# Two heads' chunk states by one whole-array product, in a retention and token-mixer kernel on one core

## The chip, the core and the metric

The kernel runs on one core of a Trainium2 chip. The metric is the device time of one execution in microseconds (us); the median of several executions is compared. A profile of one execution gives the busy time of every engine, the transfers, and which instruction waited for which. The engines are TensorE (PE; its weight loads are listed as PEld), VectorE (DVE), ScalarE (ACT), GpSimd (POOL) and SyncE (SP). They run side by side and meet at semaphores.

## The reference, cut to what matters

Four sequences (B = 4) of S = 768 tokens have H = 8 heads of D = 64 columns. The first half is a linear attention with a decay per head, the second half an MLP mixer over tokens and then over channels.

```python
gamma = 1.0 - 2.0 ** (-5.0 - np.arange(H))
for t in range(S):
    state = gamma * state + np.einsum('bhd,bhe->bhde', k[:, :, t], v[:, :, t])
    y[:, :, t] = scale * np.einsum('bhd,bhde->bhe', q[:, :, t], state)
x = y.transpose(0, 2, 1, 3).reshape(B, S, H * D)
h = np.maximum(x.transpose(0, 2, 1) @ w_tok1, 0) @ w_tok2
u = x + h.transpose(0, 2, 1)
out = u + np.maximum(u @ w_ch1, 0) @ w_ch2
```

## The kernel before, in words

**Fronts.** The 8 heads of a batch b are taken in 4 pairs p, two heads side by side in 128 columns; a pair is written (b,p) below. `front(b, p)` does one pair. The 768 tokens are 6 chunks of 128. Inside a chunk the attention is a masked 128x128 product; from chunk to chunk a 64x64 state per head is carried. The steps are, with their lines:

- k (and, in some pairs, q) is multiplied by its decay on ACT or DVE (L533, L535), and both are turned so that head columns lie on partitions: by PE (L559, L561, copied out of the bank by L569 or L574) or by a transposing transfer.
- **State products (L587 to L593).** For each of the first 5 chunks and each of the two heads, one PE product k'v of a 64x64 result (L591): 10 products into one PSUM bank. Head 0 takes the left 64 columns of the PE array and partitions 0 to 63, head 1 the right 64 columns and partitions 64 to 127. An operation that divides the array in this way has `tiled="col"`. The score products (L642) divide it by rows (`"row"`), and some of the turns of q (L559) by columns too (`"turn"`); everything else uses the whole array.
- **Recurrence (L595 to L606).** The first chunk's state is copied from the bank to U (L601, on ACT or DVE). Then four DVE steps (L603) form U[c] = decay * U[c-1] + bank[c], each 128 partitions x 64 columns, and each needs the step before it.
- U is scaled into the two diagonal blocks of `cross` (L621 on ACT or L623 on DVE, one instruction for each head).
- Score products (L642), the causal mask (L653, DVE, four instructions of 128x384 for each pair), the products with v (L673) and the products with `cross` (L699) give y in two banks. These are copied to x (L715).
- The token mixer follows: L730, its ReLU (L739 on ACT, L741 on DVE), L750, and copies to u and to X (L715); u is turned for the channel mixer (L795 with L801, or a transfer).

**Backs.** `back(b)` does the channel mixer of a batch. Batch 0 has plain products at L829. The others, and the second layer of all, use a seven-product scheme for 2x2 blocks: L898 for the first layer, L1051 and L1061 for the second, with sums on DVE (L868, L1015), copies out of a bank (L909, L1041) and adds (L918, L1068). L977 and L986 do what is left over of the last batch. At the very end one product group is cut in two halves that write the two halves of the columns of one bank (L1104); the two halves are then added to X one after the other (L1068), and stored.

**What sets the order.** Every piece of work is an `Op` with one or two ways (an engine and a planned cost each). All `Op`s are numbered as they are made. The string `ORDERED` lists these numbers, two base-62 digits each, in the planned order of start; `WAYS` has one digit for each number that picks the engine. `arrange` (L111) keeps each engine's list in that order, gives each `Op` a PSUM bank or a buffer, and L1190 to L1198 emit the instructions in the planned order. Engines run their lists strictly in order. While PE would be idle before 21 us, filler products of zeros are issued (L1196). Loads go through the POOL queue (L475, L492, L495), stores through SP or ACT (L992, L1090).

The state products need k with its decay and v (`kl + [vl, ...]`), and nothing else of the pair. The bank that holds them is free again after the last step of the recurrence. U has 2 buffers, so two pairs can be between their first copy and `cross`.

Of the kernel before, what the change touches and what calls it, by code (L numbers as in the profile page):

```python
# [9 lines left out]
FP = mybir.dt.float32  # L10
# [100 lines left out]
def arrange(ops, BANKS, seq, ways):  # L111
# [147 lines left out]
    "0e0c070d01080f05000h0306090g0i1h1i1l0m0a1j0j1k0b1m1V0n1W1v1w0k1R1x1S1y1A1T0l1z1n1U1B1o0o2r2s25261p2t1q0p292u"  # L259
    "1r2v2a1s1C0q311t322w0r1u3528331D361E1F0t1X1Y27342G1Z2K0s1G2F202x21222J2b232y2I240x1H2H2d2z2c1I0u2e2A2L2f2B2C"  # L260
    "3f2g1J0w2D3h1M1K2h2E3i1N0v372i1L2N2M382O2P392j0y1O3a2m3b2Q3g3c4L3j3d2R0D3k3e2k3l3m2S3n0A3o2n2T3p2l1P3q2W0z2U"
    "1Q3r2X2V2p0B4M3s2Z2o3t2Y3w0C303u5k3B4d3x3C3F2q490H3z4a3v3D3A4b4ead4cag3GaeaN0EaO3Eb23yaPavaf5lb30Faw3Paxah3Q"
    "aQ0Gaias3Tb4aR3SaZaSb03R0N4nb13H4p4f3Iap4qay3Jaq3Kaj4rar0Iaz4g3L3Vat3MaA4o3UaKau0R3NaLaB4h4iakaC3Oam4j4Han4k"
    "3WaE1dao3X0JaFalaH3Y02aIaD1fbhaMbk3ZaT1eaGaUaJ400MaV1gbb41be4Ibnbibc4lbp4204bo4Jbdbl430O4Kbfbm4519bjbr440Kb8"
    "461ab54mb6bsb9bg0Q1baWbaaX474s1cbPb70LaY4u4NbQ4VbJ4Obw4P4Xby4Ybx4Q4t5h5gbAbL0T5S4Rbtbz4w4S0S4v5P4ZbCbubB4xbU"
    "4W0U4Tbq4y4Ubv516q50bF0P4z5Q524A546n4DbD4B53bV5mbE555VbY4CbG4Ec5565n4F6r5T5W5i6sbK57bN5j5o5X585p5YbO48c95q59"
    "5Z5rbSbZ5s60c65Uca5u5tbMcebT5w615R5b5vcfbW5x625zc85BbXci6o5c5y6p7tc1c05D5Acj5CbR0W6t4Gc75Ecn6Y6uc25F0X6v5d6Z"
    "5a6w70cgco5G6x176V6y63ch6z5H640V5e5I655K5fcb66675J686ackcc5L6W6ccd695M6bcl5N0Y6d6Bcm5O6e6D0Z6E716fcr12cvcscM"
    "cw6g6FcNcxcA6hcycRcBcOctcS6jcucD6icUcP6kcC726CcE6m6HcTcV73cFd36lcK7u6AcH6XcWd1cL74dScId2cYcX7vdUd4cZ6G816J75"
    "117zdT7w6I7xd87A766KdX7BdVd910dZd5dY7Cczdb6Ld6e0dcdacGdWe16Mdd82e7e26Ndf84cQdi85e87De486dgdjdk7E6O77e579dl6P"  # L270
    "7y78dB7bdpdC6R7adqdm83d7dG7cds7ddHdrcpdtcJ7edndJ6Qc3dDd0dKdudI6S7ge37fdL7h7idz6U14dEdw7jdQdvdAdxdN16dR7kdedM"
    "6TdFdOe6eX15dh7lev8z7HeYdo877L7p88dPex7mdyez7K7n7IeG7F897o8Aef8aeA8Bew8CeB8beg7qeEeRcq7r7JeV7seF8cey8d8feC7G"
    "eIbH8jeWeH7M7OeJ7N8i7P7QeK13eT7ReZeN8e8g18f297eS9aeO7Sf398e9f07T8h8D8l8neL7UeD8E7Xeb7V8F9df1eU7YekeM7W80f68G"
    "ea7Z9eeled9Fec998k9f8meef48Hf78o9gc4ei9G9hbI8Ieo9if5eh9bf8f9ej9c8p8Jemepfa8q8Ken9HfdeP8Neq8r9j8Q8s8Oer8t8R8L"
    "8v8Pfh8ufyfefi9lesfzfm8w9nfDfn9mfAfEg6fffp8xfBfGfqfo9p8MfjfrfwfHfFfgfx8TfNfk8VfI8SfO8U9L9o8WfK9IfP8XfLft9Mfs"
    "fRfufQ8Y9kfCfSfUg7g89NfV8Z9r9tgb9J9O909Kg9gc9qfX9P91ge9QfY9sfW8ygfgd9ufZg49293ggg5g1fJgl9vg0gnflgmgig2949wgh"
    "gjgo96gE959xgsgagF9T9RfT9ygt9WgJ9z9X9BgKgLg39Ugvgu9VgwgM9SgGgNgpgx9AgCgHgTfv9YgOa0gU9Za1gya2gzgPgqgQgDhJa3hD"
    "gkhHgA9ChFa49EhIhOhEa5gRgIhMfMhPhKa6hNhhhSgBhGhQgrhLhlgShRhja9hmhVhTa7hihnaahWhUach1gVgZh2hYhqgXh0gWfchshrh4"
    "htgYh6h5hkethuhoabh3a8h8hphvh7hwh99DhahxhdhyhzhbhBhZeQhci3iki0i4iSilimi2i8i1i5i9ipheiri6iqibhAiaicinishCiZid"
    "fbitiieuhfifiuijiBigiwiIiCixiziDiTiGiEiUiHiXi7iVj9iYiJieiWjgiviAiKj0jsiLj1kRiQiFiNj2iRj7iOj4j8jbioj5jajqkBhg"  # L280
    "j6jejcjrktjfiPjvj3kCjhjwkujtjijyjxjjjzjojukJjkjljAjpjFjdkKjBjCjmjGk7iMihjDkvk3jEjLiyk4kwjnk5kxk8jHkLkcjMjJke"
    "jIkykfjSjQjTkdkijRkzkgkjkAk6jUkhjWjKjVkkk9jXklkDkEkakFhXjYkMkGjNkbk1kHkNkmkOjZjOkIkPjPknkQk0kqkokSk2kTkUkrkV"
    "kWkpkskXkY"
)
WAYS = (
    "000000000000000000000000000000000000000000000000000000000000000000000000000000001000000000010000000000000000"
    "100000100000001000000000000000000010110100101000000000000000000000000000010000000000000000000000000000000000"
    "110010011010001000011000000000000000000000100000000000000000000000000000000100100010000000000000000000000000"
    "001000000100000000000000000000000000000001001000000000000000000000000001100100000000000000000000000100000110"
    "010010000000000000000000000000001011001000000000000000000000000000001100100000000000000000000000000010000010"  # L290
    "000000000000000000000000000000001000000000000000010100000000101100100000100000000000000000000000000000000000"
    "000000000000000000000000000000000000000000000000000000000000001000000000000001000000000000000000000100000000"
    "000000000000011000000000000000000000000010000000000000000000000000000000001000000000100000000000000001000000"
    "000000000010000000000000000000000000000000000000000000001000000000000000000001000000000000000010000000000000"
    "000000100000000100001000000000100000000010000000000000000100010010000000000000000000000000000000010000000000"
    "000000000001100000100000000100000110000000000000000000000000000000000010100001000000100000000000000001000000"
    "000000000010010000000010000000100000001000000000000001100000000001000100010001000000000000000000000000000000"
    "00001"
# [4 lines left out]
def kernel(  # L303
# [11 lines left out]
    nc = tc.nc  # L315
# [80 lines left out]
    mask = const_p.tile([P, 1, P], FP, name="mask")  # L396
    zero = const_p.tile([P, 384], F16, name="zero")
# [106 lines left out]
    def front(b, p):  # L504
# [19 lines left out]
        def rows_of(j):  # L524
            return slice(j * D, (j + 1) * D)
# [61 lines left out]
        def emit():  # L587
            st = tile_of(ST, [P, 512], FP)
            for c in range(NC - 1):
                for j in range(2):  # L590
                    nc.tensor.matmul(st[rows_of(j), c * D:(c + 1) * D], K.tile[:, c, j], V.tile[:, j, c],  # L591
                                     start=True, stop=True)
        pp = op(one("PE", (179, 347), emit), kl + [vl, two_before], [ST], [K, V], tiled="col")  # L593

        prev = None  # L595
        for c in range(NC - 1):
            def emit(e, c=c):
                u = tile_of(US, [P, NC - 1, D], FP) if c == 0 else US.tile
                st = ST.tile[:, c * D:(c + 1) * D]
                if c == 0:  # L600
                    (nc.scalar.copy if e == "ACT" else nc.vector.tensor_copy)(u[:, 0], st)  # L601
                else:
                    nc.vector.scalar_tensor_tensor(out=u[:, c], in0=u[:, c - 1], scalar=gp[:, p:p + 1], in1=st,  # L603
                                                   op0=ALU.mult, op1=ALU.add)
            prev = op(either(emit, DVE=(190, 276)) if c else either(emit, DVE=(132, 216), ACT=act(D)), [pp, gp_op, prev], [US] if c == 0 else [],
                      ([] if c == 0 else [US]) + [ST])  # L606
# [622 lines left out]
```

## Time and profile before

| | |
|---|---|
| median of 3 runs | 186.15 us (185.56 to 186.44) |
| the profiled execution | 185.28 us, of it a span of 183.5 us in the trace |
| PE busy | 177.1 us (97%) |
| DVE busy | 168.9 us (92%) |
| ACT busy | 137.5 us (75%) |
| POOL busy | 53.8 us (29%) |
| granted PE clock | 1.00 throughout |

A row of a group of instructions reads: line, engine, operation, output<-inputs, partitions x elements and type, count, then total busy us and mean ns of one, then the idle time of that engine ahead of them and what ended it. In a timeline a row is start, length, engine, line and count of a merged run of equal instructions; a product's own length covers its way through the array, so the next product starts long before its end. In the chain of waits, each row is start, length and what the chain ran through.

### The profile page before, as it was taken

To read this page: it belongs to the slowest core of one execution; us is meant where nothing else is said; L and a number is where in the kernel's file an instruction comes from. 1 tells how busy PE (TensorE), PEld (TensorE's weight loads), DVE (VectorE), ACT (ScalarE), POOL (GpSimd) and SP (SyncE) were. 2 spreads that over 40 slices of the span, in tenths; PEclk is the share of its full clock that TensorE was granted. 3 is DMA by queue.
4 is the path that set the end of the run, shared out by engine and by line. 5 is a ranking of instruction groups with operands and counts; after the bars stand their busy time and mean duration, and the time that the engine had idled before them with its cause. 6 is when DMAs were issued, how large, how long until landed. Compare 5 with 4: busy or idle time off the path is not lost.

```text
span 183.5 us, 5308 instructions
## 1 busy us (share of the span) xinstructions
PE 177.1 (97%) x2089; PEld 133.9 (73%) x2089; DVE 168.9 (92%) x450; ACT 137.5 (75%) x320; POOL 53.8 (29%) x63
## 2 busy tenths in 40 slices
PE   7789999999999999999999999999999999999993
PEld 3455898566789988866668899767778986566893
DVE  5699999989999899999999999998999989889893
ACT  6667899547979998899999896899975455688100
POOL 8997586553508008604051220000000000000000
PEclk9999999999999999999999999999999999999999
DMA  6999999999999999999999799702602333610046
GB/s 121 153 173 182 179 187 201 178 193 206 168 155 160 154 162 152 160 153 131 132 211 121 200 118 187 176 0 42 90 2 46 88 126 120 229 57 0 4 184 218
DMA packets 94137, 25.31 MB, mean 138 GB/s; under 512 B 83616, under 2 KB 91296, under 8 KB 94112
## 3 DMA queue, kind: packets, MB, share of 16 engines
q0 software_dynamic: 67728, 13.18, 85.6%
q1 hardware_dynamic: 24656, 9.31, 23.9%
q10 hardware_dynamic: 1728, 2.49, 4.0%
q8 instruction: 16, 0.26, 0.5%
q14 instruction: 9, 0.07, 0.1%
HBM read 26.74 MB, written 6.29 MB: 180 GB/s over the span
## 4 chain that ended last, share of the span: by engine, by line
PE 86%; POOL 5%; DMA 5%; DVE 2%; issue 0%; POOLq 0%
PE bank L898 22%; PE bank L1051 16%; PE bank L1061 12%; PE bank L829 9%; PE bank L750 6%; PE bank L730 6%; DMA wt<-in_moe_w_tok_dram 5%; PE bank L642 3%; PE bank L977 3%; PE bank L673 3%; PE bank L699 2%; PE bank L591 2%; POOL v L495 2%; POOL k L495 2%; POOL q L492 2%; PE bank L795 1%
## 5 line engine op out<-in xcount | busy, mean ns | idle before, releaser
L653 DVE TENSOR_TENSOR am<-bank,mask 128x384 f16<-128x384 f32 x64 | 32.9, 546 | 0.8 <-PE bank L642 0.8
L918 DVE TENSOR_TENSOR h<-bank,us 128x384 f16<-128x384 f32 x54 | 29.2, 550 | 1.7 <-PE bank L898 1.2
L909 ACT COPY us<-bank 128x384 f32<-128x384 f32 x51 | 23.4, 482 | 7.6 <-PE bank L898 7.2
L495 POOL DMA_DIRECT2D v<-in_v_dram x16 | 16.5, 1035 | 39.8 <-PE bank L699 17.9
L898 PE MATMUL bank<-hs,late 128*128 128x384 f16 x108 | 22.4, 326 | 0.0
L1068 DVE TENSOR_TENSOR X<-X,bank 128x256 f32<-128x256 f32 (+1 forms) x45 | 17.9, 405 | 2.1 <-PE bank L1061 1.7
L1051 PEld LDWEIGHTS <-hs 128*128 128x128 f16 x192 | 17.9, 98 | 2.5
L1041 ACT COPY us<-bank 128x256 f32<-128x256 f32 x27 | 9.9, 369 | 13.0 <-PE bank L1051 11.2
L898 PEld LDWEIGHTS <-late 128*128 128x128 f16 x144 | 13.2, 98 | 7.9 <-DVE hs L868 0.7
L603 DVE SCALAR_TENSOR_TENSOR U<-U,gp,bank 128x64 f32<-128x64 f32 x64 | 16.8, 272 | 1.1 <-ACT U L601 0.5
L1051 PE MATMUL bank<-wsum,hs 128*128 128x256 f16 x132 | 17.6, 273 | 0.0
L829 PE MATMUL bank<-uT,wc 128*128 128x384 f16 x96 | 17.2, 326 | 0.0
L621 ACT ACTIVATE cross<-U,gp 64x320 f16<-64x320 f32 x28 | 15.6, 558 | 2.0 <-DVE U L603 1.7
L495 POOL DMA_DIRECT2D k<-in_k_dram x15 | 15.4, 1026 | 4.9 <-DVE kT L574 2.1
L898 PE MATMUL bank<-uT,wc 128*128 128x384 f16 x72 | 16.3, 326 | 0.0
L750 PE MATMUL bank<-h,wt 128*128 128x128 f16 x192 | 15.0, 219 | 0.0
L715 ACT CAST x<-bank 128x384 f16<-128x384 f32 x31 | 14.7, 490 | 0.4 <-PE bank L699 0.4
L845 ACT ACTIVATE h<-bank 128x384 f16<-128x384 f32 x24 | 10.9, 503 | 5.2 <-PE bank L829 5.1
L898 PEld LDWEIGHTS <-wc 128*128 128x128 f16 x108 | 10.0, 98 | 5.8 <-issue 0.2
L1061 PEld LDWEIGHTS <-h 128*128 128x128 f16 x132 | 12.4, 98 | 2.0 <-DVE h L925 0.6
L750 PEld LDWEIGHTS <-wt 128*128 128x128 f16 x192 | 12.3, 98 | 1.8
L715 ACT COPY X<-bank 128x384 f32<-128x384 f32 x28 | 13.5, 496 | 0.0
(96 smaller groups left out, 393.7 us busy)
## 6 DMA issues: line engine op xcount, KB each, us to landing
out_dram<-X SPq DMA_DIRECT2D x14, 256.0 KB, 2.4
q<-in_q_dram POOLq DMA_DIRECT2D x16, 192.0 KB, 5.9
v<-in_v_dram POOLq DMA_DIRECT2D x16, 192.0 KB, 6.5
k<-in_k_dram POOLq DMA_DIRECT2D x15, 192.0 KB, 6.5
wc<-in_moe_w_ch_dram POOLq DMA_DIRECT2D x5, 512.0 KB, 13.9
out_dram<-X ACTq DMA_DIRECT2D x8, 256.0 KB, 2.6
wc<-in_moe_w_ch_dram POOLq DMA_DIRECT2D x2, 256.0 KB, 9.4
us<-in_k_dram SPq DMA_DIRECT2D x1, 384.0 KB, 3.4
```

Of the source, the lines that this page charges most:

```text
L495: (nc.sync if hard else nc.gpsimd).dma_start(out=tile_of(s, [P, 2, NC, D], FP if hard else F16), in_=src.rearrange("h (c p) d -> p (h c) d ...
L603: nc.vector.scalar_tensor_tensor(out=u[:, c], in0=u[:, c - 1], scalar=gp[:, p:p + 1], in1=st, op0=ALU.mult, op1=ALU.add)
L653: nc.vector.tensor_tensor(am, SC[g].tile[:, :m * P].rearrange("p (i t) -> p i t", t=P), mask.to_broadcast([P, m, P]), ALU.mult)
L715: (nc.scalar.copy if e == "ACT" else nc.vector.tensor_copy)(tile(), t)
L750: nc.tensor.matmul(Y[j].tile[:, 2 * i * D:2 * (i + 1) * D], wt2[:, jt, t], H1.tile[:, jt], start=False, stop=(jt == NJ - 1), skip_group_ch ...
L829: nc.tensor.matmul(acc[:, :SH], wc1[:, ct, ft * P:(ft + 1) * P], UT.tile[:, ct, sh * SH:(sh + 1) * SH], start=(ct == 0), stop=(ct == NP - 1))
L898: nc.tensor.matmul(acc[:, :SH], left(ct), r[:, ct], start=first and ct == 0, stop=ct == C2 - 1, skip_group_check=True)
L909: (nc.scalar.copy if e == "ACT" else nc.vector.tensor_copy)(ks[:, j], R1.tile[:, :SH])
L918: nc.vector.tensor_tensor(h(m, sh), R.tile[:, :SH], KS.tile[:, j], ALU.add)
L1051: nc.tensor.matmul(acc_[:, lo], l[:, j], r[:, j], start=first and j == 0, stop=j == K2 - 1, skip_group_check=True)
L1061: nc.tensor.matmul(acc_[:, lo], l[:, j], r[:, j], start=first and j == 0, stop=j == K2 - 1, skip_group_check=True)
L1068: (nc.vector if e == "DVE" else nc.gpsimd).tensor_tensor(dst(), dst(), b_(), ALU.add)
```

## The change

1. **State products.** One product for each chunk takes k of both heads (128 columns) as weights and v of both heads (128 columns) as the moving operand. It uses the whole array, `tiled` is gone, and 5 products stand in place of 10. The result is 128x128 in fp32; the two 64x64 blocks on its diagonal are the states, the other two blocks are not used.
2. **One bank has room for four of them.** The first four are issued together. The fifth goes into the columns of the first, so it is an `Op` of its own that depends on the copy of the first state to U, and the fifth recurrence value waits for it.
3. **Recurrence over 128 columns.** U is 128 columns wide for each chunk; the first copy and the four DVE steps run over 128 columns in place of 64. `cross` reads the diagonal blocks (64 columns with a stride of 128).
4. **Mask and zeros.** The mask is f16 in place of fp32, and the zero tile of the filler is 128 columns read three times in place of 384.
5. **A new order.** `ORDERED` and `WAYS` are new (1317 `Op`s in place of 1301).

The core of the diff:

```diff
-    mask = const_p.tile([P, 1, P], FP, name="mask")
-    zero = const_p.tile([P, 384], F16, name="zero")
+    mask = const_p.tile([P, 1, P], F16, name="mask")
+    zero = const_p.tile([P, 1, P], F16, name="zero")
...
         def emit():
-            st = tile_of(ST, [P, 512], FP)
-            for c in range(NC - 1):
-                for j in range(2):
-                    nc.tensor.matmul(st[rows_of(j), c * D:(c + 1) * D], K.tile[:, c, j], V.tile[:, j, c],
-                                     start=True, stop=True)
-        pp = op(one("PE", (179, 347), emit), kl + [vl, two_before], [ST], [K, V], tiled="col")
+            states(range(NC - 2))
+
+        def states(cs):
+            st = tile_of(ST, [P, 512], FP) if cs[0] == 0 else ST.tile
+            for c in cs:
+                nc.tensor.matmul(st[:, c % 4 * P:(c % 4 + 1) * P], K.tile[:, c].rearrange("p h d -> p (h d)"), V.tile[:, :, c],
+                                 start=True, stop=True)
+        pp = op(one("PE", (216, 384), emit), kl + [vl, two_before], [ST], [K, V])
...
-                u = tile_of(US, [P, NC - 1, D], FP) if c == 0 else US.tile
-                st = ST.tile[:, c * D:(c + 1) * D]
+                u = tile_of(US, [P, NC - 1, P], FP) if c == 0 else US.tile
+                st = ST.tile[:, c % 4 * P:(c % 4 + 1) * P]
...
+            if c == NC - 2:
+                pp = op(one("PE", (60, 222), lambda: states([NC - 2])), [pp, u0], [], [ST, K, V])
...
+            u0 = prev if c == 0 else u0
...
-                    u, g = US.tile[rows_of(j)], gp[rows_of(j), p:p + 1]
+                    u, g = US.tile[rows_of(j), :, rows_of(j)], gp[rows_of(j), p:p + 1]
...
-                    nc.tensor.matmul(spare[:, :384], zero[:, :P], zero, start=True, stop=True)
+                    nc.tensor.matmul(spare[:, :384], zero[:, 0], zero.to_broadcast([P, 3, P]), start=True, stop=True)
```

Decoded with the numbering above, the new strings say this:

- On PE's list the array changes between whole, rows and columns 42 times in place of 65. From the first L730 product on it is 31 in place of 48: 20 changes to or from the column-divided state products are gone, and 3 between rows and the whole array came in their place.
- Ahead of the first L730 product stand the same `Op`s as before, the fifth products of (0,0) and (0,1), and one more run of six products with v (L673). The ten loads asked for ahead of `w_tok1` on the POOL queue are the same ten, in another order.
- Counted by kind, ten decays of k or q move from DVE to ACT. Seven further `Op`s move to ACT (two copies of x or u, one `cross`, one ReLU of L741, two of L925, one first copy of U), and ten move to DVE (four copies of L909, two of L801, one of L574, two ReLUs of L954, one copy of L1041).
- The places, in the planned order, of the fifth product and of the recurrence step of the same pair next ahead of it (c = 0 is the copy):

| pair | step ahead | its place | fifth product | | pair | step ahead | its place | fifth product |
|---|---|---|---|---|---|---|---|---|
| (0,0) | c = 0 | 40 | 43 | | (2,0) | c = 2 | 416 | 427 |
| (0,1) | c = 0 | 70 | 73 | | (2,1) | c = 2 | 496 | 497 |
| (0,2) | c = 2 | 101 | 102 | | (2,2) | c = 0 | 564 | 587 |
| (0,3) | c = 2 | 135 | 137 | | (2,3) | c = 2 | 629 | 630 |
| (1,0) | c = 1 | 184 | 206 | | (3,0) | c = 0 | 766 | 774 |
| (1,1) | c = 2 | 259 | 260 | | (3,1) | c = 0 | 815 | 818 |
| (1,2) | c = 3 | 329 | 331 | | (3,2) | c = 2 | 856 | 857 |
| (1,3) | c = 1 | 400 | 407 | | (3,3) | c = 3 | 949 | 955 |

- In the last product group that is cut in two (L1104), the second half stood ahead of the add of the first half (places 1288 and 1289); now it stands behind it (1303 and 1302).

More of the change, by code (lines that the diff above doesn't have):

```diff
@@ L264 @@
[L264 to L268, printed above, removed]
@@ L279 @@
[L279 to L283, printed above, removed]
+    "0e0107080d050f000h030b090c0g060m1h1i0n1l1m0i1j1k0a0k1W1x1X1w0j1S1z1T1y1B0l1n1U1A1o1C1V1s1p1D0o1q1r271t2x0p29"
```

67 lines of the change are left out of this document (38 added, 29 removed).

## The prediction

> **What bounds the kernel now.** I read the page's busy lines first, then the chain of waits, then the busy times by stretch.
>
> ```profile
> span 183.5 us, 5308 instructions
> PE 177.1 (97%) x2089; PEld 133.9 (73%) x2089; DVE 168.9 (92%) x450; ACT 137.5 (75%) x320; POOL 53.8 (29%) x63
> PE 86%; POOL 5%; DMA 5%; DVE 2%; issue 0%; POOLq 0%
> ```
>
> TensorE is busy for 97% and makes up 86% of the chain that ended last. The rest of the chain lies at three places. In the chain in order of time:
>
> ```profile
> 10.69 8.28 DMA wt<-in_moe_w_tok_dram
> 19.01 0.84 PE bank L730 x12
> ...
> 93.15 1.00 DVE h L918 x2
> ...
> 95.31 0.59 DVE h L925
> ...
> 180.53 0.29 DVE X L986
> ```
>
> Until 19.01 us the chain is POOL issuing loads and the load of `w_tok1`. From there to 180.53 it is PE, broken once for long, by four rows of DVE work from 93.15 to 95.90 (two of them shown). Then comes the last add and its store. By stretch:
>
> ```profile
> 0.00:19.00 19.00, 15.94 (x198) 8.99 (x198) 14.54 (x59) 12.98 (x23) 16.42 (x24) 1.00 1.61 158
> 61.00:76.00 15.00, 14.98 (x225) 13.28 (x224) 14.09 (x41) 14.25 (x35) 5.10 (x6) 1.00 1.59 157
> 91.00:106.00 15.00, 14.72 (x179) 11.44 (x177) 15.00 (x40) 13.39 (x33) 4.58 (x5) 1.00 1.14 170
> 106.00:121.00 15.00, 14.96 (x192) 12.26 (x190) 15.00 (x41) 12.68 (x33) 0.51 (x1) 1.00 1.05 147
> sum 183.50, PE 177.08 PEld 133.95 DVE 168.92 ACT 137.51 POOL 53.81; mean PE 14.76 PEld 11.16 DVE 14.08 ACT 11.46 POOL 4.48
> ```
>
> After the length come PE, PEld, DVE, ACT, POOL and the granted clock (1.00). PE has hardly a gap, and DVE is full from 91 to 121. So PE time after 19 us counts in full, a wait of PE counts in full, and DVE time counts only where PE ends up waiting for it.
>
> **The state products.** In PE's timeline, a group of ten between whole-array neighbours, and two groups back to back:
>
> ```profile
> 75.90 0.44 PE L730 MATMUL bank<-x,wt 128*128 128x128 f16 x5
> 76.27 0.35 PE L591 MATMUL bank<-v,k 128*64 128x64 f16 x10
> 76.55 0.82 PE L898 MATMUL bank<-uT,wc 128*128 128x384 f16 x4
> ...
> 59.90 0.33 PE L699 MATMUL bank<-cross,qT 128*128 128x128 f16 x3
> 60.16 0.51 PE L591 MATMUL bank<-v,k 128*64 128x64 f16 x20
> 60.60 0.50 PE L1061 MATMUL bank<-wsum,h 128*128 128x256 f16 x3
> ```
>
> For an ordinary whole-array run and two other runs, from the chain:
>
> ```profile
> 25.28 0.35 PE bank L673 x12
> 37.34 0.43 PE bank L591 x20
> 57.61 0.67 PE bank L730 x12
> ```
>
> Twelve whole-array products of 128 columns take 0.67 us, 0.056 each. Five L730 products of 0.44 us in all start four times 0.056 apart, so the last starts at 76.12; L898 starts at 76.55. Less the 0.056 of that last product, ten column-divided products cost 0.37 us, of it some 0.2 for the two changes of the array. The same reckoning gives 0.53 for twenty. The new form costs 5 x 0.056 = 0.28 for a pair.
>
> After 19 us there are thirteen pairs, by PE's timeline in ten groups. Five stand alone like the first group: -0.09 each, -0.46. Two doubles like the second: +0.03 each. Three groups touch a score block, whose own change of the array stays: two single ones I count at nothing, and the double at 37.34 costs 0.43 against 0.56, +0.13. One fifth product that falls behind the first L730 adds 0.06. The sum is -0.46 + 0.06 + 0.13 + 0.06 = **-0.21 us**. One run of six L673 products moves ahead of the wait for `w_tok1`, half of the 0.35 row: **-0.17**.
>
> The Trainium skill (TensorEngine Tiling (Array Packing), Theoretical Speedup) promises up to twice the speed for a dimension of 64 or less, which speaks against giving the division up; its Key Properties say that a change of mode drains the array. By the first alone the ten products would double from about 0.17 to 0.34, +2.2 us for thirteen pairs. By the rows they grow to 0.28, and the changes that go pay it back.
>
> **The wait that the fifth product adds.** It goes into the bank that the steps c = 1 to 3 read, in other columns. The last rows of the timeline show how instructions on two halves of one bank stand to each other:
>
> ```profile
> 179.10 0.83 PE L1104 MATMUL bank<-wc,hs 128*128 128x128 f16 x12
> 179.30 0.42 DVE L1068 TENSOR_TENSOR X<-X,bank 128x256 f32<-128x256 f32 x1
> ...
> 179.97 0.48 DVE L1068 TENSOR_TENSOR X<-X,bank 128x128 f32<-128x128 f32 x2 [0.25 <-PE bank L1104]
> ```
>
> The first six of these twelve products write the first half, and the sixth ends at about 179.60 (five starts of 0.056 behind 179.10, and one product's length, 0.83 less eleven starts, 0.22). DVE is free at 179.72, yet its add of that half starts at 179.97, when the twelfth has ended at 179.93. The waits go by bank, not by columns. If they do so in the other direction too, the fifth product waits for every step of its pair emitted ahead of it, and everything on PE's list stands behind it.
>
> The Trainium skill (PSUM — Partial Sum Buffer, PSUM bank collisions raise a hardware error) asks for the same: guard by bank and quadrant, not by address. The 0.25 us row agrees.
>
> The step's cost, and those of the other changed instructions, in the groups by form:
>
> ```profile
> L603 DVE SCALAR_TENSOR_TENSOR U<-U,gp,bank 128x64 f32<-128x64 f32 x64 | 16.8, 272 | 1.1 <-ACT U L601 0.5
> L601 DVE COPY U<-bank 128x64 f32<-128x64 f32 x5 | 1.1, 217 | 0.1
> L601 ACT COPY U<-bank 128x64 f32<-128x64 f32 x11 | 2.6, 238 | 0.9 <-PE bank L591 0.9
> L1068 DVE TENSOR_TENSOR X<-X,us 128x512 f32<-128x512 f32 x11 | 7.5, 682 | 0.2
> L1068 DVE TENSOR_TENSOR X<-X,us 128x256 f32<-128x256 f32 x11 | 4.5, 414 | 0.0
> L909 DVE COPY us<-bank 128x384 f32<-128x384 f32 x3 | 1.7, 554 | 0.5 <-PE bank L898 0.5
> L909 ACT COPY us<-bank 128x384 f32<-128x384 f32 x51 | 23.4, 482 | 7.6 <-PE bank L898 7.2
> L535 DVE TENSOR_SCALAR k<-k,gk 128x384 f16<-128x384 f16 x13 | 4.4, 346 | 0.3 <-DMA k<-in_k_dram 0.3
> L533 ACT ACTIVATE k<-k,gk 128x384 f16<-128x384 f16 x17 | 10.3, 615 | 1.4 <-DMA k<-in_k_dram 1.3
> L653 DVE TENSOR_TENSOR am<-bank,mask 128x384 f16<-128x384 f32 x64 | 32.9, 546 | 0.8 <-PE bank L642 0.8
> L569 DVE TENSOR_TENSOR qT<-bank,late 128x768 f16<-128x768 f16 x8 | 7.5, 944 | 1.5 <-ACT k L533 0.9 <-PE bank L559 0.6
> ```
>
> Between 256 and 512 columns an add grows by 268 ns, 1.05 a column, so a step grows by 67 ns to 0.34 us. By the decoded order seven pairs have the fifth product one place (five of them) or two places behind such a step. A place is about 183.5/1301 = 0.14 us. If both engines keep to the order, PE waits 0.34 - 0.14 = 0.20 five times and 0.06 twice, 1.1 us. In the tail the second half of L1104 now stands behind the add of the first, some 0.28 long: another 0.14. The ends are nothing (the steps are done when PE gets there, or the waits don't bind in this direction) and 7 x 0.34 + 0.28 = 2.7. I take **+1.0**, below the sum because the first wait loosens those near it.
>
> The fifth product's named dependency, the copy of the first state, is covered after 19 us: two pairs start there with a whole run of L730 (0.67) or two half runs and more in between, the others with more, against 0.22 for a product and about 0.3 for the copy.
>
> **DVE and ACT.** 64 steps grow by 67 ns, +4.3 us; four copies left on DVE, +0.3. Ten decays leave, 0.35 each, -3.5. Of the other moves ten come (nine near the 0.55 of a 384-column copy, one 0.4: +5.4) and seven go (three near 0.55, the others 0.2 to 0.4: -2.9). DVE ends at about +3.6 on 168.9, inside 183.5. ACT takes ten decays (0.615, +6.2), twelve copies wider by 0.06 (+0.7; 482 against 238 over 320 columns is 0.76 ns a column, so 0.05 to 0.06), and the rest nearly cancels: some 142, far from full. I count both at nothing on the path: the decays leave as much as the wider steps bring, and PE work hides them. If that cover is gone, see the second rival.
>
> **The rest, at nothing.** The f16 mask: L653 has an fp32 bank on the other side; L569 mixes a 16-bit bank and an fp32 operand and needs (944 - 546)/384 = 1.04 ns for each further column, the pace of the adds. A mixed pair gains nothing there; were it faster, the gain would be DVE time, which the path doesn't hold. The zero tile and filler end before 19.01, hidden by the load, and the same ten loads stand ahead of `w_tok1`. The longer hold of the bank and of U: no wait for either stands in the chain; between 0 and 0.3 us, taken as 0. Loads for later batches come in another order, and the work that uses them is moved with them; 0, and at worst PE once waits for about one load, 1.0 by the issue row below. Stores: two more on ACT, the last one on SP as before; 0.
>
> ```profile
> L495 POOL DMA_DIRECT2D k<-in_k_dram x15 | 15.4, 1026 | 4.9 <-DVE kT L574 2.1 <-DVE U L603 1.5 <-ACT x L715 0.7
> L730 PEld LDWEIGHTS <-wt 128*128 128x128 f16 x192 | 11.7, 98 | 1.6 <-DMA wt<-in_moe_w_tok_dram 0.5 <-issue 0.2
> ```
>
> **Sum.** -0.21 - 0.17 + 1.0 = +0.6. The profiled execution took 185.28 (1.8 around its span), so 185.9. The median of the runs is 0.87 above that execution: **186.8 us**.
>
> **Rivals.**
> - *The waits don't bind.* PE keeps its -0.38 alone: 185.28 - 0.38 + 0.87 = 185.8; if the new order also fills the stall from 93 to 96 (0.28 of PE idle in that stretch) and some of the small ones around it, 184.8 to 185.5. For it: in the chain PE waits for DVE at one place only, so DVE is mostly ahead. Against it: the table of places, and the 0.25 us row.
> - *VectorE becomes the bound.* Place: 91 to 121, where it has 15.00 of 15.00 twice. Price: at least the wider steps of four pairs, 4 x 4 x 0.067 = 1.1, at most the whole 3.6, on PE's 185.8: 186.9 to 189.4, say 188.2. It decides once PE waits for L653, L918 or L603 in sum longer than the 0.28 of now by a microsecond. Against it: PE idles only 0.32 in these 30 us although DVE is full, so DVE's order still runs ahead of PE there.
> - *The new products don't run at 0.056.* With each weight load of 0.098 in the open, a pair takes 0.49, +0.21 for each of thirteen on the forecast: 189.5. Against it: L730 has the same shape and the same loads, and does 0.056.
>
> **How the numbers follow.** Forecast, waits of 0.4 to 1.7 us: chance 0.43, own range 186.2 to 187.5. First rival: 0.36, of it 0.17 below 185.2. VectorE: 0.16. Slow products: 0.05. The range leaves out the last, half of the VectorE case and the lowest 0.06: 184.8 to 188.2. Runs of this kernel tell 0.5% from no change, which is 185.2 and 187.1 here. Faster by more: 0.17. Within: 0.19 of the first rival and 0.29 of the forecast, 0.48. Slower: 0.14 of the forecast and the two other rivals, 0.35.
>
> **What would show it.** Five products start 0.056 apart and no gap stands around them; the fifth product has PE idle ahead of it, released by L603 or L601, 0.1 to 0.3 us in the pairs (0,2), (1,1), (2,1), (2,3), (3,2); L603 has a mean near 340; the first L730 still starts near 19.0; L653 stays at 546. Wrong would be: no PE wait on L603 at all, or PE waits on L653 and L918 that grow past a microsecond.

## The result, and the profile after

The changed kernel takes 190.62 us (median of 6 runs, 189.75 to 191.94); the kernel before, on the same chip, 185.86 (median of 6, 185.12 to 186.44). The ratio is 1.0267, with a 95% interval of 1.0237 to 1.0297: slower by 2.7%, outside the forecast's range. The profiled execution took 190.84 us. Its page, the same lines as were read of before:

```profile
span 188.9 us, 5143 instructions
PE 179.7 (95%) x2010; PEld 136.3 (72%) x2010; DVE 174.9 (93%) x443; ACT 139.1 (74%) x327; POOL 53.8 (28%) x63
PE 49%; DVE 28%; DMA 10%; ACT 8%; issue 3%; POOL 1%; DVEq 0%; POOLq 0%; ACTq 0%
```

TensorE's share of the chain that ended last fell from 86% to 49%, and VectorE's rose from 2% to 28%. DVE is busy for 6.0 us more than before, not for the 3.6 of the forecast. By stretch (length, then PE, PEld, DVE, ACT, POOL and the granted clock; DMA's share and GB/s stand last):

```profile
61.00:76.00 15.00, 14.28 (x186) 12.54 (x184) 14.54 (x39) 12.17 (x31) 5.49 (x6) 1.00 1.34 125
91.00:106.00 15.00, 14.10 (x165) 10.19 (x163) 14.75 (x35) 13.86 (x36) 4.05 (x4) 1.00 1.71 166
106.00:121.00 15.00, 14.57 (x187) 13.03 (x187) 14.76 (x40) 13.35 (x33) 1.01 (x1) 1.00 1.00 160
```

Before the change PE was busy for 14.98, 14.72 and 14.96 in these stretches. It now loses 0.7, 0.9 and 0.4 us in them, with DVE all but full beside it and the clock at 1.00. What PE waits for after 19 us (waits of PE; total us, times, longest), first before the change, then after:

```profile
PE bank L1061 <- DVE h L925: 0.3, 1, 0.3
```

```profile
PE bank L593 <- DVE U L605: 2.4, 6, 0.7
PE bank L1056 <- DVE X L1073: 0.8, 1, 0.8
PE bank L735 <- DVE kT L574: 0.2, 1, 0.2
PE bank L903 <- DVE h L923: 0.2, 1, 0.2
```

All four are waits for VectorE. Lines have moved: the state products are L593 (from L591), the first copy to U is L603 (L601), the steps L605 (L603), mask L658, scores L647, channel-mixer products L903, L1056 and L1066, the adds to X L1073, ReLUs L930. The groups of the changed instructions, by form, and of the decays that stayed on DVE:

```profile
L593 PE MATMUL bank<-v,k 128*128 128x128 f16 x80 | 9.7, 219 | 2.5 <-DVE U L605 2.4
L605 DVE SCALAR_TENSOR_TENSOR U<-U,gp,bank 128x128 f32<-128x128 f32 x64 | 21.5, 341 | 1.7 <-PE bank L593 1.0
L658 DVE TENSOR_TENSOR am<-bank,mask 128x384 f16<-128x384 f32 x64 | 32.2, 547 | 0.6 <-PE bank L647 0.6
L535 DVE TENSOR_SCALAR k<-k,gk 128x384 f16<-128x384 f16 x7 | 3.3, 473 | 0.0
L535 DVE TENSOR_SCALAR q<-q,gy 128x384 f16<-128x384 f16 x5 | 1.9, 371 | 0.0
```

A step takes 0.341 us (forecast 0.34) and the mask 0.547 (before 0.546): both sizes were right. The largest wait shows how the loss comes about. PE's timeline around the fifth product of pair (2,1), then DVE's:

```profile
72.55 0.83 PE L735 MATMUL bank<-x,wt 128*128 128x128 f16 x12
74.11 0.23 PE L593 MATMUL bank<-v,k 128*128 128x128 f16 x1 [0.72 <-DVE U L605]
74.17 0.82 PE L1066 MATMUL bank<-wsum,hs 128*128 128x256 f16 x6
```

```profile
72.42 0.78 DVE L535 TENSOR_SCALAR k<-k,gk 128x384 f16<-128x384 f16 x1
73.13 0.33 DVE L605 SCALAR_TENSOR_TENSOR U<-U,gp,bank 128x128 f32<-128x128 f32 x1
73.38 0.41 DVE L1073 TENSOR_TENSOR X<-X,bank 128x256 f32<-128x256 f32 x1
73.71 0.34 DVE L605 SCALAR_TENSOR_TENSOR U<-U,gp,bank 128x128 f32<-128x128 f32 x1
74.37 0.35 DVE L605 SCALAR_TENSOR_TENSOR U<-U,gp,bank 128x128 f32<-128x128 f32 x1 [0.33 <-PE bank L593]
```

The fifth product could start at 73.22, after the last of the twelve L735. It starts at 74.11, when the step c = 2 (73.71 to 74.05) has ended. That step is a place ahead of it in the planned order, as the forecast's table says, but DVE doesn't reach it in time: a decay of 0.78 us, a step and an add come first. Then the next step waits in turn for the fifth product. Start to start, less the length of the work ahead, PE loses 0.22, 0.46, 0.62, 0.40, 0.89, 0.45 and 0.59 us at the fifth products of (0,2), (0,3), (1,1), (1,2), (2,1), (2,3) and (3,2). These are the seven pairs named in the forecast, and no other pair after 19 us loses anything; but the sum is 3.6 us, not 1.1. (The list of waits has 2.4 of it, since PE still counts as busy while the product ahead runs through the array.)

### The profile page after: what moved, and what is told of

The parts are those of the page before. It is cut to its first block, busy times and chain, and to the rows that moved or that the text cites. A ratio compares the mean times of both kernels' runs of the same rounds, so it can differ in the third digit from the quotient of the medians.

```text
span 188.9 us, 5143 instructions
## 1 busy us (share of the span) xinstructions
PE 179.7 (95%) x2010; PEld 136.3 (72%) x2010; DVE 174.9 (93%) x443; ACT 139.1 (74%) x327; POOL 53.8 (28%) x63
## 4 chain that ended last, share of the span: by engine, by line
PE 49%; DVE 28%; DMA 10%; ACT 8%; issue 3%; POOL 1%; DVEq 0%; POOLq 0%; ACTq 0%
PE bank L903 19%; PE bank L1056 8%; DMA wc<-in_moe_w_ch_dram 7%; PE bank L1066 7%; DVE X L1073 6%; DVE am L658 6%; DVE U L605 4%; DVE hs L1020 4%; PE bank L735 3%; PE bank L755 3%; DMA q<-in_q_dram 2%; PE bank L982 2%; DVE late L1174 2%; DVE h L923 2%; ACT x L720 2%
## 5 line engine op out<-in xcount | busy, mean ns | idle before, releaser
L658 DVE TENSOR_TENSOR am<-bank,mask 128x384 f16<-128x384 f32 x64 | 32.2, 547 | 0.6 <-PE bank L647 0.6
L923 DVE TENSOR_TENSOR h<-bank,us 128x384 f16<-128x384 f32 x54 | 28.6, 551 | 0.2
L914 ACT COPY us<-bank 128x384 f32<-128x384 f32 x47 | 21.8, 484 | 8.5 <-PE bank L903 6.9
L605 DVE SCALAR_TENSOR_TENSOR U<-U,gp,bank 128x128 f32<-128x128 f32 x64 | 21.5, 341 | 1.7 <-PE bank L593 1.0
L903 PE MATMUL bank<-hs,late 128*128 128x384 f16 x108 | 22.9, 326 | 0.2 <-DVE h L923 0.2
L1056 PEld LDWEIGHTS <-hs 128*128 128x128 f16 x192 | 18.3, 98 | 2.3
L903 PEld LDWEIGHTS <-late 128*128 128x128 f16 x144 | 13.3, 98 | 7.9 <-issue 0.4
L1073 DVE TENSOR_TENSOR X<-X,bank 128x256 f32<-128x256 f32 (+1 forms) x45 | 17.8, 407 | 1.0 <-PE bank L1066 0.7
L834 PE MATMUL bank<-uT,wc 128*128 128x384 f16 x96 | 18.6, 326 | 0.0
L626 ACT ACTIVATE cross<-U,gp 64x320 f16<-64x320 f32 x29 | 16.2, 559 | 3.1 <-DVE U L605 2.7
L1056 PE MATMUL bank<-wsum,hs 128*128 128x256 f16 x132 | 17.7, 273 | 0.0
L903 PE MATMUL bank<-uT,wc 128*128 128x384 f16 x72 | 16.6, 326 | 0.0
L720 ACT CAST u<-bank 128x384 f16<-128x384 f32 x31 | 14.9, 489 | 1.6 <-PE bank L755 1.1
L903 PEld LDWEIGHTS <-wc 128*128 128x128 f16 x108 | 9.9, 98 | 5.5 <-issue 0.3
L533 ACT ACTIVATE k<-k,gk 128x384 f16<-128x384 f16 x23 | 13.7, 618 | 0.2
L735 PE MATMUL bank<-x,wt 128*128 128x128 f16 x192 | 13.4, 219 | 0.2 <-DVE kT L574 0.2
L1066 PEld LDWEIGHTS <-h 128*128 128x128 f16 x132 | 12.5, 98 | 1.5
```

What stands on the lines that cost most here:

```text
L658: nc.vector.tensor_tensor(am, SC[g].tile[:, :m * P].rearrange("p (i t) -> p i t", t=P), mask.to_broadcast([P, m, P]), ALU.mult)
L720: (nc.scalar.copy if e == "ACT" else nc.vector.tensor_copy)(tile(), t)
L735: nc.tensor.matmul(acc[:, jt * P:(jt + 1) * P], wt1[:, i, jt * P:(jt + 1) * P], X16.tile[:, i].rearrange("p h d -> p (h d)"), start=(i == ...
L903: nc.tensor.matmul(acc[:, :SH], left(ct), r[:, ct], start=first and ct == 0, stop=ct == C2 - 1, skip_group_check=True)
L914: (nc.scalar.copy if e == "ACT" else nc.vector.tensor_copy)(ks[:, j], R1.tile[:, :SH])
L923: nc.vector.tensor_tensor(h(m, sh), R.tile[:, :SH], KS.tile[:, j], ALU.add)
```

## The experiments

Three theories stood after the result. **The wait**: the forecast's mechanism, only larger, so that without a fifth product in a read bank the kernel is back at the time of before. **The width**: VectorE, with steps of 128 columns, has become the bound, so that steps of 64 columns bring the time back, waits or not. **The order**: the new order costs time by itself. Ratios are to the kernel before on the same chip, with 95% intervals; 1% is 1.86 us. A difference of two ratios has the errors of both: about 0.5%, 0.9 us, and 1.2 us where e14 is one of the two.

### e1_no_fifth, e3_narrow, e8_no_fifth_narrow: two causes, each alone and both

e1 against the changed kernel:

```diff
-                pp = op(one("PE", (60, 222), lambda: states([NC - 2])), [pp, u0], [], [ST, K, V])
+                pp = op(one("PE", (60, 222), lambda: None), [pp, u0], [], [ST, K, V])
```

> The changed kernel without its fifth product: nothing is issued in its place, and the step c = 4 reads the state of chunk 0 again, so the fifth state is left out of the computation. All instructions of VectorE stay. Theory A (TensorE waits by bank): the 3.6 us that TensorE spent idle ahead of the seven fifth products go, less what shows up elsewhere: 186.5 to 188 us, and no wait of the products on L605. Theory B (VectorE is the bound with its wider steps): the waits turn up ahead of other products, above all those with v and the second-layer products; 189.5 to 190.5.

e3 against the changed kernel:

```diff
-                u = tile_of(US, [P, NC - 1, P], FP) if c == 0 else US.tile
-                st = ST.tile[:, c % 4 * P:(c % 4 + 1) * P]
+                u = tile_of(US, [P, NC - 1, D], FP) if c == 0 else US.tile
+                st = ST.tile[:, c % 4 * P:c % 4 * P + D]
...
-                    u, g = US.tile[rows_of(j), :, rows_of(j)], gp[rows_of(j), p:p + 1]
+                    u, g = US.tile[rows_of(j)], gp[rows_of(j), p:p + 1]
```

> The changed kernel with a recurrence over the left 64 columns of each product alone, so head 1's states are not the right block. The products and the order stay as they are; the first copy and the 64 steps are as short as before the change. Theory A: the seven waits shrink by one to three shorter steps each, 0.5 to 1.4 us in sum: 189 to 190. Theory B: 4.3 us of VectorE's work are gone, and with them most of the loss: 186 to 187.5.

e8 has both edits.

> The changed kernel with both left out: no fifth product, and a recurrence over the left 64 columns alone (the fifth state and head 1's states are not computed). Each alone gave some 188.4 us. If the two losses are separate and add up, 186 to 186.5 us. If both act on the same wait, 187.5 to 188.4 us, and what is left is the new order's own loss.

| kernel | median us | ratio to before |
|---|---|---|
| changed kernel | 190.62 | 1.0267 (1.0237 to 1.0297) |
| e1, no fifth product | 188.43 | 1.0125 (1.0089 to 1.0160) |
| e3, steps of 64 columns | 188.34 | 1.0126 (1.0085 to 1.0167) |
| e8, both | 186.24 | 1.0008 (0.9980 to 1.0036) |

Either edit takes back half of the loss, and both take back all of it. So neither the wait nor the width is the cause alone; within the error their prices add. The fifth product is worth 1.42% with wide steps (1.0267 less 1.0125) and 1.18% with narrow ones, 2.2 to 2.6 us. Of that 0.8 is no wait: fourteen fifth products after 19 us do 0.056 each. The width is worth 1.41% with and 1.17% without the fifth product, again 2.2 to 2.6 us. PE's largest waits on DVE after 19 us, in e1, e3 and e8:

```profile
PE bank L1056 <- DVE X L1073: 0.8, 1, 0.8
PE bank L800 <- DVE U L605: 0.6, 1, 0.6
...
PE bank L593 <- DVE h L923: 0.3, 1, 0.3
PE bank L903 <- DVE h L923: 0.3, 1, 0.3
```

```profile
PE bank L1056 <- DVE X L1073: 0.8, 1, 0.8
PE bank L593 <- DVE U L605: 0.6, 1, 0.6
```

```profile
PE bank L1056 <- DVE X L1073: 0.8, 1, 0.8
```

With wide steps and no fifth product, PE waits for DVE elsewhere: the turn of u (L800) needs a bank that late steps still read, and two products need a bank or sums that L923 hands over late. With narrow steps these waits are gone. Where the fifth product is there, narrow steps bring PE's loss at the seven pairs from 3.6 to 1.8 us: half of that loss was the width too.

### e2_own_bank, e11_later_fifth: the wait taken away with nothing left out

In e2 the fifth product has a bank of its own (against the changed kernel):

```diff
+        S5 = Slot(FA)
...
-            st = tile_of(ST, [P, 512], FP) if cs[0] == 0 else ST.tile
+            st = tile_of(ST if cs[0] == 0 else S5, [P, 512], FP)
...
-                st = ST.tile[:, c % 4 * P:(c % 4 + 1) * P]
+                st = (S5 if c == NC - 2 else ST).tile[:, c % 4 * P:(c % 4 + 1) * P]
...
-                pp = op(one("PE", (60, 222), lambda: states([NC - 2])), [pp, u0], [], [ST, K, V])
+                pp = op(one("PE", (60, 222), lambda: states([NC - 2])), [pp, u0], [S5], [K, V])
```

> The changed kernel with the fifth product in a PSUM bank of its own, taken from the same eight; nothing is left out. Theory A: as without the fifth product, 186.5 to 188 us, since the bank that the steps read is no longer written. Theory B: 189.5 to 190.5. If the banks are what is short, TensorE waits for a bank elsewhere and the time is not below 190.

In e11 the product stays in that bank, but `ORDERED` has it four to seven places behind the step c = 3, and the last step two places behind it or more; its `Op` names that step as a dependency (`[pp, u0, prev]`).

> The changed kernel with each fifth product moved behind the step c = 3 of its pair by five to seven places in the order, and the last step two places behind it; it names that step as a dependency. Nothing is left out, the bank is shared as in the change. Theory A: TensorE finds the steps done, the seven waits go from 3.6 us to under 1: 187.5 to 189 us. Theory B: the wait only moves, 190 to 191 us.

e2: 193.00 us, 1.0361 (1.0308 to 1.0415). e11: 193.04 us, 1.0359 (1.0303 to 1.0415). Both are slower than the changed kernel. PE's largest waits after 19 us, e2 (lines two higher: L737 token mixer, L1058 channel mixer, L607 steps, L1075 adds) and e11:

```profile
PE bank L737 <- DVE U L607: 0.8, 1, 0.8
PE bank L1058 <- DVE U L607: 0.8, 1, 0.8
PE bank L1058 <- DVE X L1075: 0.8, 1, 0.8
PE bank L680 <- DVE X L1075: 0.5, 1, 0.5
```

```profile
PE bank L800 <- DVE U L605: 0.9, 1, 0.9
PE bank L1056 <- DVE X L1073: 0.8, 1, 0.8
PE bank L834 <- DVE U L605: 0.4, 1, 0.4
```

In neither is a fifth product seen to wait for a step any more, and in both some other product waits for a bank that the steps read for longer. The wait at the fifth product is one place where PE feels that DVE is late; taken away there, it turns up at the next product that needs one of the banks. So, as these rows read, "no fifth product" is cheaper in e1 because the work and one user of the bank are gone, not because a wait can be moved away. That is argued, not shown: neither edit takes away the wait alone. By the planned costs in its own code, `arrange` ends at 187.3 us for e2 and for e11, and at 182.2 for the changed kernel, so by plan, too, the order suits them less.

### e13_products_old_order, e14_products_wide_old_order: products and width without any fifth wait

Both keep the old order and issue all five whole-array products in one go; the fifth writes over the fourth. Against the kernel before, e13 (with f16 mask and short zero tile as well):

```diff
-                    nc.tensor.matmul(st[rows_of(j), c * D:(c + 1) * D], K.tile[:, c, j], V.tile[:, j, c],
-                                     start=True, stop=True)
-        pp = op(one("PE", (179, 347), emit), kl + [vl, two_before], [ST], [K, V], tiled="col")
+                nc.tensor.matmul(st[:, min(c, 3) * P:(min(c, 3) + 1) * P], K.tile[:, c].rearrange("p h d -> p (h d)"), V.tile[:, :, c],
+                                 start=True, stop=True)
+        pp = op(one("PE", (276, 444), emit), kl + [vl, two_before], [ST], [K, V])
...
-                st = ST.tile[:, c * D:(c + 1) * D]
+                st = ST.tile[:, min(c, 3) * P:min(c, 3) * P + D]
```

> The order of before with five whole-array products for each pair issued in one go and a recurrence over 64 columns. The fifth product overwrites the fourth's columns, so the state of chunk 3 and head 1's states are left out; nothing waits that did not wait before. This measures the product term alone. By the prediction's sum 0.2 to 0.3 us less than before: 185.9 to 186.1 us, within the error. If the whole-array products cost their weight loads, 188.5 us or more; if the changes of the array cost more than counted, 184.5 to 185.5 us.

e14 against e13:

```diff
-                u = tile_of(US, [P, NC - 1, D], FP) if c == 0 else US.tile
-                st = ST.tile[:, min(c, 3) * P:min(c, 3) * P + D]
+                u = tile_of(US, [P, NC - 1, P], FP) if c == 0 else US.tile
+                st = ST.tile[:, min(c, 3) * P:(min(c, 3) + 1) * P]
```

> As the run with the products alone in the old order, and the recurrence over 128 columns (the state of chunk 3 is still left out). The difference to that run is the width alone, without a fifth product that waits. If VectorE's fullness sets the price, 1.5 to 3 us more, since the old order moves no decays to ScalarE; if width costs only where a product waits for the steps, under 1 us more.

e13: 186.03 us, 0.9990 (0.9964 to 1.0017). e14: 188.45 us, 1.0112 (1.0055 to 1.0168). The new products give about what the forecast gave them: -0.2 us, with an interval from -0.7 to +0.3 that takes in zero. In e13's PE timeline the five start 0.28 us ahead of their successor, which is 5 x 0.056:

```profile
77.30 0.44 PE L593 MATMUL bank<-v,k 128*128 128x128 f16 x5
77.58 0.65 PE L900 MATMUL bank<-uT,wc 128*128 128x384 f16 x3
```

The width costs 1.22%, 2.3 us, in an order that has no fifth wait at all. The page's busy lines of e13 and e14:

```profile
PE 178.6 (97%) x2008; PEld 136.2 (74%) x2008; DVE 169.0 (92%) x450; ACT 137.2 (74%) x320; POOL 53.7 (29%) x63
```

```profile
PE 179.8 (96%) x2009; PEld 136.5 (73%) x2009; DVE 173.0 (92%) x450; ACT 138.0 (74%) x320; POOL 53.8 (29%) x63
```

4.0 us more of DVE cost 2.3 us of the whole, with DVE at 92% of the span: about half of it lands on the path (2.3 has an error of 1.2). The waits of e14 tell only a part of where. The largest is in e14's PE timeline, where a group of score products waits for a bank that late masks still read:

```profile
121.69 0.51 PE L644 MATMUL bank<-qT,kT 64*128 64x128 f16 x12 [0.58 <-DVE am L655]
```

Start by start, PE in e14 is 0.8 us behind e13 at the first token-mixer product (20.83 against 20.01), 1.4 at 31 us, 1.9 at 91 and 2.7 at 122, and no further behind after that. Up to 24 us e14's chain of waits holds six steps of 0.35 to 0.36 us, e13's none.

### e15_less_relu: is it the chain of the steps, or VectorE's load?

The width lengthens the recurrence and also fills DVE. e15 keeps the wide steps and takes other work off DVE (against the changed kernel, L930):

```diff
-                            nc.vector.tensor_scalar(h(m, sh), h(m, sh), 0.0, None, ALU.max)
+                            pass
```

> The changed kernel without the in-place ReLUs that VectorE does (33 instructions, 5.5 us at one every 0.167 us; that part of the channel mixer is left out). Steps and fifth products stay. If VectorE's fullness makes the steps late, taking other work off it helps as much as narrow steps did: 187 to 188.5 us, and the waits ahead of the fifth products fall. If the length of each step and its chain is the price, 189.5 to 190.5 us and the waits stay.

188.59 us, 1.0130 (1.0086 to 1.0173). DVE is busy for 168.3 us, 6.6 less than in the changed kernel (the 5.5 of the expectation was the planned cost), and the time falls by 1.37%, 2.5 us, as much as narrow steps give with 3.9 less (171.0 in e3). PE's largest wait after 19 us:

```profile
PE bank L593 <- DVE U L605: 1.9, 5, 0.7
```

The fifth waits stay nearly whole (3.1 of the 3.6 us, start to start), but the wait of L1056 for an add is gone. The expectation's two cases are thus mixed: the time is that of the case of a full DVE, the waits are those of the case of the chain. Work that has nothing to do with the steps is worth as much as their width, so DVE's load counts. The run doesn't exclude that the length of the steps' chain counts besides: a us of ReLUs seems to bring less (2.5 of 6.6) than a us of steps (2.6 of 3.9). In the changed kernel that wait stands here, first PE's timeline, then DVE's and POOL's:

```profile
102.76 0.82 PE L1056 MATMUL bank<-wc,h 128*128 128x256 f16 x6 [0.78 <-DVE X L1073]
```

```profile
98.22 1.67 DVE L930 TENSOR_SCALAR h<-h 128x384 f16<-128x384 f16 x4
...
101.20 0.72 DVE L930 TENSOR_SCALAR h<-h 128x384 f16<-128x384 f16 x1
...
102.30 0.41 DVE L1073 TENSOR_TENSOR X<-X,bank 128x256 f32<-128x256 f32 x1
```

```profile
97.78 1.01 POOL L495 DMA_DIRECT2D v<-in_v_dram  x1 [8.19 <-PE bank L903]
98.78 3.05 POOL L495 DMA_DIRECT2D k<-in_k_dram  x3
```

Five ReLUs stand ahead of the add that frees the bank; without them the wait doesn't arise. They are slow here: elsewhere a ReLU takes 0.25 us and the next starts 0.17 behind it, so four would take 0.75 and the fifth 0.25. They take 1.67 and 0.72, 1.4 us more (an estimate from these numbers), beside four issues of loads on POOL. The last section comes back to this.

### e10_order_alone, e5_before_mask_zero, e6_old_order: the rest

e10 is the kernel before with the new `ORDERED` and `WAYS`, their entries for the fifth products taken out and the numbers closed up.

> The kernel before with the new order and choice of engines alone, the entries of the fifth products taken out; products, recurrence, mask and zero tile as before. It has the changes of the array of the old products. Theory A and B: within 0.5% of before, 185.5 to 187.5 us. If the order itself costs (the first token-mixer product later, a second-layer product waiting for an add of X): 187.5 to 189 us.

187.93 us, 1.0086 (1.0055 to 1.0117). Its PE waits after 19 us hold the 0.8 of the channel mixer's wait for an add (L1056 on L1073 in the changed kernel):

```profile
PE bank L1051 <- DVE X L1068: 0.8, 1, 0.8
```

So the new order costs 1.6 us with the old products. This one wait, which the kernel before, e13 and e14 don't have, is as long as half of it, and the five ReLUs stand ahead of it here too (1.67 and 0.71 us, beside issues of loads). e8 gives a second figure. It has the new order and products, and is at +0.1 us although it saves the fifth products' 0.8 and the 0.2 of the product term: about 1.1.

e5 is the kernel before with the mask and the zero tile of the change:

```diff
-    mask = const_p.tile([P, 1, P], FP, name="mask")
-    zero = const_p.tile([P, 384], F16, name="zero")
+    mask = const_p.tile([P, 1, P], F16, name="mask")
+    zero = const_p.tile([P, 1, P], F16, name="zero")
```

> The kernel before with the f16 mask and the short zero tile of the filler alone. Theories A and B: no change, 185.3 to 186.6 us, and the mask instruction stays at 546 ns. Theory C (the filler that reads one 128-column tile three times keeps TensorE's clock low for longer at the start, so that the first token-mixer product comes late): 1 to 1.6 us slower, with the full clock granted near 10 us instead of 4.

186.36 us, 0.9993 (0.9954 to 1.0031), and the mask takes 547 ns: no change, as forecast, to within 0.9 us. The expectation's third theory was that the short zero tile keeps TensorE slow for longer at the start. Three filler products in PE's timelines of the kernel before, of e5 and of e1, which has the short tile too:

```profile
6.80 0.65 PE L1196 MATMUL bank<-zero 128*128 128x384 f16 x3
```

```profile
7.30 1.17 PE L1196 MATMUL bank<-zero 128*128 128x384 f16 x3
```

```profile
6.80 0.65 PE L1201 MATMUL bank<-zero 128*128 128x384 f16 x3
```

In every trace the first fillers start 0.32 us apart, though the clock column reads 1.00 there, and later ones 0.16. The later pace is first seen at 4.3 us in the kernel before and at 4.4 in e1, at 6.9 to 7.7 in e3, e6, e8 and e15, and at 10.0 to 10.4 in the changed kernel, e2, e5, e11, e13 and e14. e10, with the long tile, has it at 4.0 and falls back (granted clock 0.56 from 7 to 10 us). So the tile alone doesn't fix this moment; what does is open.

e6 takes the old order with everything else of the change; the fifth product has a bank of its own and stands right behind the first four (e2's edits, with `[pp]` for `[pp, u0]`).

> The order of before with the new products and the wide recurrence: each fifth product stands directly behind the first four of its pair, in a bank of its own, so it waits for no step. Theory A (bank waits plus the new order): near the kernel before, 185.5 to 187 us. Theory B (wider steps on VectorE, with no decay moved away): VectorE has 4.6 us more and nothing taken off it; 188 to 190 us, with TensorE waiting for VectorE in front of products that did not wait before. If the extra bank is what costs, TensorE waits for banks, as with the own bank in the new order.

199.99 us, 1.0745 (1.0669 to 1.0821), the slowest of all. Its largest PE wait after 19 us:

```profile
PE bank L737 <- DVE U L607: 1.9, 1, 1.9
```

A group of the token mixer's first-layer products waits there for a bank that steps still read. e14, with the same order, the same width and the same place of the fifth product, differs by having one bank for each pair, and is 11.5 us faster. So the price is that of the second bank; the run says nothing for or against the width or the wait.

## Why the prediction was wrong

The step that failed is **"I count both at nothing on the path: the decays leave as much as the wider steps bring, and PE work hides them."** Measured, the wider steps alone cost 2.2 to 2.6 us, as DVE is full and PE doesn't hide them. The other errors are smaller. By its own terms:

- **Products, -0.21 and -0.17.** The five start 0.056 apart, and e13 is at -0.2 us, with an interval that takes in zero; so the first term agrees. The second has no run of its own: the six products did move ahead of the first L735, but that came later, not earlier.
- **Wait of the fifth product, +1.0.** The mechanism was right: waits go by bank in this direction too, at the seven pairs of the table and nowhere else. The size was too small: 2.2 to 2.6 us for the fifth product, less its own 0.8, is 1.4 to 1.8. The working gave the step a head start of one place, 0.14 us, "If both engines keep to the order"; DVE came late, and PE lost 3.6 us there. With narrow steps it loses 1.8, not far from the 1.1 that was worked out. The time lost by the whole is smaller than 3.6. Without the fifth products other waits open (about 1 us in e1's rows above), so part of the 3.6 would be lost elsewhere; that a pause at one product loosens the waits behind it, as the forecast assumed, is argued from this.
- **DVE and ACT, 0.** Measured 2.2 to 2.6 us for the width, in both orders (e8 to e1, e3 to the changed kernel, e13 to e14). Besides, DVE's sum was off: +6.0 us in place of +3.6. The steps brought 4.7 (4.3 was worked out). The ten decays that left were to take 3.5 along, but decays on DVE fell only from 7.4 to 6.1, since those that stayed take 473 and 371 ns where the price was 346 and 320, and the one of the fp32 k 877 where it was 421 (876 to 992 in e1, e13 and e14 too).
- **The new order, 0.** It costs 1.1 to 1.6 us by itself (with an error of 0.6 to 0.9), and L1056's wait for an add, 0.8, is as long as half of that. The forecast looked for stalls that the order might fill, and not for ones that it might open.
- **Mask, zero tile, 0.** No run speaks against it (e5, to within 0.9 us).
- **The start.** The first L735 came at 20.61 us, not near 19.0, ahead of it 0.22 of waiting for DVE's kT. I don't settle how much of it is the change: e5, with before's code but for mask and zeros, starts it at 19.72, e8 at 19.59, e13 at 20.01 and e10 at 20.53. Part is within the 1.1 to 1.6 of the order and the price of the width: the changed kernel's chain of waits runs to this product through DVE from 10.39 on, with five steps in it from 12.62 to 18.00, where the chain before ran through the load of `w_tok1`. Part may be the slow pace of TensorE up to 10.0 us, where the kernel before had the later pace from 4.3 and e1 from 4.4. The forecast's row for 0 to 19 hides how little room DVE had here: before the change it was busy for 8.59 of the last 9.00 us of that stretch.

The sum with measured terms is -0.2 + 1.1 to 1.6 + 2.2 to 2.6 + 1.4 to 1.8, 4.5 to 5.8 us, and 2.67% is 5.0. Its lower end closes by construction, as the 1.1 was worked out from e8 with the other terms; only e10's 1.6 and e14's 2.3 are measured apart.

Of the rivals, "VectorE becomes the bound" came nearest. Its price, 1.1 to 3.6 us, holds the 2.2 to 2.6 that were measured; its place, 91 to 121, was too narrow, since in e14 half of the loss is there by 31 us. Its sign, a microsecond more of waiting for L653, L918 or L603, couldn't tell it from the forecast, whose own wait is one for L603. The argument against it, 0.32 us of PE idle in these 30 us although DVE was full, was read as slack. It was the edge: with DVE at 15.00 of 15.00 there and close to full elsewhere, about half of what was given to it landed on PE. And forecast and rival were set against each other as two cases, one of which would hold. The four runs of the first experiment show that they held together.

What stays open: how much the change loses at the start, and how e2 and e11 come to be 2.4 us slower than the changed kernel. Their waits are shown, but no run takes them apart. No version among these that does the whole computation beats the kernel before.

## What to carry to other kernels

An engine that is full in a stretch has no slack there, even if the bound engine doesn't wait for it yet: price work given to it at about half its length (2.3 us of 4.0, 2.6 of 3.9 and 2.5 of 6.6 here) unless a row shows where it can go. A product into unused columns of a bank that another engine reads waits for the whole bank, and a second bank need not help (193.0 us against 190.6 here). An order fitted to one set of lengths is a change of its own, to be measured with the old instructions (1.6 us here).

## What the runs showed of the hardware

A decay on DVE that runs beside POOL's issue of a load can take three times as long. The same decay, in e1 and in e8, DVE's timeline and then POOL's of each:

```profile
72.32 0.92 DVE L535 TENSOR_SCALAR q<-q,gy 128x384 f16<-128x384 f16 x1
```

```profile
72.11 2.05 POOL L495 DMA_DIRECT2D q<-in_q_dram  x2
```

```profile
71.83 0.31 DVE L535 TENSOR_SCALAR q<-q,gy 128x384 f16<-128x384 f16 x1
```

```profile
71.82 2.05 POOL L495 DMA_DIRECT2D q<-in_q_dram  x2
```

It depends on where in the issue the decay falls. In e1 it starts 0.21 us behind the issue's start and ends 0.08 behind the end of the first of the two loads; in e8 it starts 0.01 behind and takes its 0.31. The thirteen traces have one pattern for the f16 decays and ReLUs on DVE:

| where it starts | how many | what it takes |
|---|---|---|
| beside no issue of a load | 445 | 0.24 to 0.32 us |
| up to 0.18 us behind the start of an issue | 32 | 0.24 to 0.32 us |
| 0.29 to 0.70 us behind it | 68 | 0.39 to 0.82 us: each ends 0.05 to 0.09 behind the issue's end |

Between 0.19 and 0.28 us both are seen, and behind 0.70 little of the issue is left. In the changed kernel every decay on DVE over 0.4 us lies for nearly its whole length beside such an issue (0.78 at 72.42, the one ahead of the late step). This is why the decays that stayed cost more than those of before, and why the five ReLUs ahead of L1056's wait take 1.4 us more. When POOL issues depends on PE in turn: the issue at 97.78 had waited for PE, as its row says. Over 0.31 us for a decay and 0.25 for a ReLU, such rows come to 3.3 us in the changed kernel and 1.9 before, an estimate from the traces; the difference is a part of the 6.0 that DVE has more. In e1 the 0.92 stands right ahead of the step for whose bank L800 waits, so that wait is partly chance; the price of the width rests on the medians. The cause is argued from these rows; no experiment moved a load away from a decay. The Trainium skill (SBUF — State Buffer, SBUF: two separate sides) says that VectorE's fast modes and GpSimd share a pair of ports under an exclusive lock. The 68 rows agree with that, in the direction in which VectorE is the one that waits; the 32 rows show no wait in the first 0.18 us of an issue.
